# A fused attention and two feed-forward layers: another order of the first batch's ten attention groups

## Chip, cores and metric

One core of a Trainium2 chip runs the whole program. The metric is device time in microseconds (us), from the first to the last instruction of one execution. The engines are TensorE (PE; PEld is its weight load), VectorE (DVE), ScalarE (ACT), GpSimd (POOL), and SyncE (SP), which here only issues transfers.

## The reference

Attention with two kinds of heads (four look back 32 positions, four look at every 32nd position), then two gated feed-forward layers; only the first of them normalises its input.

```python
scores = q @ k^T / sqrt(64)                      # 4 batches, 8 heads, 576 positions, head width 64
mask_local   = (rel >= 0) & (rel < 32)           # heads 0..3
mask_strided = (rel >= 0) & (pos_k % 32 == pos_q % 32)   # heads 4..7
x = softmax(where(mask, scores, -1e9)) @ v       # as 2304 tokens of width 512
xn = x / sqrt(mean(x*x) + 1e-6) * rms_g
y = (silu(xn @ w_gate) * (xn @ w_val)) @ w_out   # 512 -> 1536 -> 512
out = (silu(y @ w_gate2) * (y @ w_val2)) @ w_out2
```

## The kernel before

**Attention.** A batch is worked in ten groups: five strided (numbers 0 to 4) and five local (5 to 9). Local groups 5 and 6 hold tokens 0 to 255 of the batch for the two pairs of heads, 7 and 8 hold tokens 256 to 511, 9 holds the last 64. Each group has three steps, in the diff called s, t and v. The step s (`local_s`, `strided_s`, `softmax_step`) makes the scores on PE, then the masked scores and row maxima on DVE (line 677), the exponentials on ACT (line 686), sums and reciprocals on DVE (lines 696 and 697) and the normalised tile `e` on POOL (line 703). The step t (`turn_step`) turns `e` on PE (line 80) and copies it to the tile `pT` on ACT (line 87). The step v (`local_v`, `strided_v`) multiplies by v on PE and copies the result to the token tile `x` on ACT (line 87).

**Normalisation.** `rms_step` makes the sums of squares over features of a piece of tokens on PE (`ones,ss`), the mean on DVE (868), the root on POOL (871), diagonal tiles `dg` on DVE (876), a broadcast on PE (`dg,ones`) and the scaled tokens on DVE (887). For batch 0 the first piece is its first 256 tokens (called r0 in the diff), the second the other 320 (r1). The first piece is then split into a high and a low part (`split`: `xh` on ACT at 998, `xl` on DVE at 999), and the feed-forward layer starts with segment 0, these 256 tokens.

**Order.** `batch` writes the steps as one list. Per place i of its loop it takes the scores of group i, the turn of group i-3 and the product of group i-4, so that three scores steps stand between the scores of a group and its turn. The loop `point` starts one step of the list at each of its calls, lets running steps advance by one phase, and between them starts phases of the weights' preparation. For a weight tile that is: load to `raw` (line 160), two ACT operations (288 and 280), two DVE operations (292 and 297), then a rounded half on ACT (305) and the rest on DVE (309). PE work is kept in the order written by hand (`traced`); ACT, DVE, POOL and SP are ordered by a scheduler from priorities.

**Fillers.** In the start phase `keep_busy` sets a given number of matmuls of a constant tile (`b_v<-warm`, line 72) ahead of some PE groups. Nothing uses their result. A table gives their number by the group's count.

**After the start.** Feed-forward chunks of segment 0 (gate `b_g<-xh,w`, value `b_v<-xh,w`, line 76) alternate on PE with the steps of batch 1, which came into the list behind batch 0. `silu` works on ACT at 975 and on DVE at 976; `hidden` is at 983 to 987.

Of the kernel before, what the change touches and what calls it, by code (L numbers as in the profile page):

```python
# [25 lines left out]
def attn_ffn_ffn(ctx: ExitStack, tc: tile.TileContext, q, k, v, w1g, w1v, w1o, rms_g, w2g, w2v, w2o, out):  # L26
# [7 lines left out]
    HC = FC // 3  # L34
# [32 lines left out]
    def keep_busy():  # L67
        if state["start"] and state["kind"] and state["group"] != state["filled"]:
            state["filled"] = state["group"]
            state["count"] += 1  # L70
            for _ in range({1: 26, 11: 34, 14: 16, 20: 6, 27: 8, 28: 5, 31: 7, 34: 9, 36: 22, 40: 2, 43: 5}.get(state["count"], 0)):
                traced(nc.tensor.matmul(att.fill, att.warm[:, :128], att.warm, start=True, stop=True))

    def product(out_, a, b_, start, stop, **how):
# [24 lines left out]
    state = {"rate": 640000.0, "slack": 0, "late": False, "xr": 0.6, "early": False, "start": True, "hold": False, "kind": "", "group": 0, "filled": 0, "count": 0, "lag": 3, "wait": 4}  # L99
# [211 lines left out]
    def weight_step(m, c, z, park=False):  # L311
        cell = {}
# [30 lines left out]
        def save():  # L343
# [5 lines left out]
            spent(cell["bk"], 6)  # L349
            parked[m, c, z] = d  # L350

        return Step([load] + [wait] * ((6, 6, 10, 6)[c] if (m, c) < (1, HC) else 0) + scale(cell, int(not park)) + ([high, low, save] if park else [first, second]),
                    lambda: (park or room[4]) and spaces() >= 1, PRIO_W)

    QUARTERS = ((1, 2), (5, 6), (7, 4), (3,))
# [139 lines left out]
    class Attention:  # L495
# [407 lines left out]
        def batch(self, b):  # L903
            groups = []
# [5 lines left out]
                               self.local_v(b, tiles, {3 if b else 1: 1, 4: 2}.get(i, 0))))  # L910
            res = []
            n = len(groups)
            for i in range(n + 4):
                if i == 0:
                    res += [self.strided_t(b, w, p, w and p == 2) for p in range(3) for w in range(2)]
                if i == 5:
                    res += [self.local_t(b, w, 0) for w in range(2)]
                if i == 5 + 0:
                    res += [self.local_t(b, w, 1) for w in range(2)] + [self.local_rest(b)]
                if i < n:  # L920
                    res.append(groups[i][0])
                if 0 <= i - 3 < n:
                    res.append(groups[i - 3][1])
                if 0 <= i - 4 < n:
                    res.append(groups[i - 4][2])
                    if i - 4 in (8 if b else 6, 9):
                        res.append(self.rms_step(b, int(i - 4 == 9)))
            return res

# [656 lines left out]
    for n, (m, cs, t0) in enumerate(work):  # L1586
# [54 lines left out]
        if n == 0:  # L1641
            cell = stage_x(nxt[0], nxt[2])
# [6 lines left out]
        for i, c in enumerate(chunks[:-1]):  # L1649
            c1 = chunks[i + 1]  # L1650
            step(c1, 1)
            if i == 0 and n and nxt:
                while due:
                    due.pop(0)[2]()
                cell = stage_x(nxt[0], nxt[2])
# [67 lines left out]
```

## Time and profile before

| | us |
|---|---|
| runs of before (three) | 999.80, 1001.33, 1003.00; median 1001.33 |
| profiled execution, its own time | 1004.73 |
| its span from first to last instruction | 1002.9 |
| PE busy in that span | 974.3 (97%) |
| ACT busy, DVE busy | 576.3, 580.5 |
| first feed-forward matmul on PE | 51.87 after the start |

The page of the profile divides the span into 40 slices of 25 us; the first two hold what the change touches. Within them the order of the single instructions on each engine counts, so the timelines of the engines are read, and a table of busy time by stretch.

### The profile page before, as it was taken

Reading aid. Unit: us, or ns where it says so; the run is one execution under the profiler, and the core shown is the slowest. Engines: PE = TensorE matmul, PEld = TensorE weight load, DVE = VectorE, ACT = ScalarE, POOL = GpSimd, SP = SyncE. Lnnn points to the kernel's source line nnn. Section 1 sums busy time; section 2 is a strip of 40 time slices with the busy share of each in tenths; the row PEclk is TensorE's granted clock in tenths of the full one; section 3 lists DMA queues with packets and bytes.
Section 4 is the critical chain, followed back from the end, with each engine's and each line's share of the span. In section 5 each row is a group of like instructions: output and inputs, shape, how many; then the busy total and the mean of one; then the engine's idle time right before and its main releaser. Section 6 shows DMA issues by size and latency. Waiting matters only on the chain.

```text
span 1002.9 us, 17802 instructions
## 1 busy us (share of the span) xinstructions
PE 974.3 (97%) x6054; PEld 897.0 (89%) x6054; DVE 580.5 (58%) x1319; ACT 576.3 (57%) x1465; POOL 387.4 (39%) x416
## 2 busy tenths in 40 slices
PE   9889998899999999899999999999999999999998
PEld 8778876678989999899999998999998999999997
DVE  5777768757335656356646657544556555663333
ACT  7988786755345645356555546555656645553431
POOL 3121254531221628161634565571516243441500
PEclk9989999999999999899999999999999999999999
DMA  7774669658684665887758685557887397955211
GB/s 199 225 214 141 165 188 265 207 190 286 225 290 153 208 201 190 309 269 240 247 178 280 232 253 219 186 188 274 288 281 260 110 327 242 324 179 168 88 60 63
DMA packets 168455, 215.89 MB, mean 215 GB/s; under 512 B 46860, under 2 KB 122028, under 8 KB 168364
## 3 DMA queue, kind: packets, MB, share of 16 engines
q1 hardware_dynamic: 158559, 199.48, 61.2%
q10 hardware_dynamic: 9805, 15.27, 4.2%
q8 instruction: 48, 0.79, 0.3%
q14 instruction: 43, 0.35, 0.1%
HBM read 142.87 MB, written 71.83 MB: 214 GB/s over the span
## 4 chain that ended last, share of the span: by engine, by line
PE 70%; DMA 4%; ACT 2%; DVE 1%; issue 0%; SPq 0%; DVEq 0%
PE b_y L76 32%; PE b_a L76 17%; PE b_g L76 12%; PE b_v L76 10%; DMA pk<-dh 1%; DMA w<-pk 1%; DMA raw<-in_moe_w_gate_dram 1%; DMA pk<-raw 0%; DMA xraw<-x_d 0%; SPq L160 0%; DMA part<-ob 0%; ACT xh L1395 0%; ACT dh L280 0%; DMA x_d<-x 0%; DVE dh L297 0%
## 5 line engine op out<-in xcount | busy, mean ns | idle before, releaser
L1396 POOL TENSOR_TENSOR xl<-xst,xh 128x384 fp32r<-128x384 f32 x196 | 211.3, 1099 | 178.8 <-PE b_y L76 77.7
L76 PE MATMUL b_y<-xh,w 128*128 128x384 f32 x784 | 211.6, 335 | 2.3 <-ACT t L1453 1.2
L76 PEld LDWEIGHTS b_y<-xh,w 128*128 128x128 f32 x784 | 142.9, 188 | 5.4 <-ACT t L1453 1.8
L76 PE MATMUL b_a<-xh,w 128*128 128x384 f32 (+2 forms) x512 | 141.1, 335 | 0.8 <-ACT t L1453 0.8
L76 PE MATMUL b_y<-xl,w 128*128 128x384 f32 x392 | 131.4, 335 | 0.0
L76 PE MATMUL b_g<-xh,w 128*128 128x384 f32 (+2 forms) x416 | 128.2, 350 | 1.2 <-DVE sg L976 1.2
L76 PE MATMUL b_v<-xh,w 128*128 128x384 f32 (+2 forms) x352 | 108.7, 352 | 3.6 <-ACT t L1467 3.6
L76 PEld LDWEIGHTS b_a<-xh,w 128*128 128x128 f32 x512 | 93.3, 188 | 4.1 <-ACT t L1453 1.8
L1395 ACT CAST xh<-xst 128x384 fp32r<-128x384 f32 x196 | 91.5, 520 | 0.0
L386 POOL TENSOR_TENSOR raw<-dh 128x256 f32<-128x256 f32 x40 | 29.4, 754 | 154.0 <-DVE dh L297 55.4
L76 PE MATMUL b_a<-xl,w 128*128 128x384 f32 (+2 forms) x256 | 85.9, 335 | 0.0
L76 PEld LDWEIGHTS b_g<-xh,w 128*128 128x128 f32 x416 | 77.8, 192 | 6.8 <-DVE sg L976 1.4
L76 PE MATMUL b_y<-hh,w 128*128 128x384 f32 (+2 forms) x304 | 81.4, 343 | 0.0
L76 PEld LDWEIGHTS b_y<-xl,w 128*128 128x128 f32 x392 | 73.6, 188 | 1.8
L76 PEld LDWEIGHTS b_v<-xh,w 128*128 128x128 f32 x352 | 65.5, 192 | 9.0 <-ACT t L1467 3.9
L76 PE MATMUL b_g<-xl,w 128*128 128x384 f32 (+2 forms) x208 | 70.8, 340 | 0.0
L703 POOL TENSOR_TENSOR e<-e,rc 128x384 f32<-128x384 f32 (+3 forms) x40 | 37.4, 940 | 84.3 <-DVE rc L697 15.9
L76 PE MATMUL b_y<-w,hh 128*128 128x512 f32 x216 | 67.1, 391 | 0.0
L686 ACT ACTIVATE e<-e,nb 128x96 f32<-128x96 f32 (+2 forms) x152 | 57.3, 386 | 8.0 <-DVE nb L677 8.0
L76 PE MATMUL b_v<-xl,w 128*128 128x384 f32 (+2 forms) x176 | 59.9, 340 | 0.0
L76 PEld LDWEIGHTS b_y<-hh,w 128*128 128x128 f32 x304 | 55.3, 190 | 2.8 <-ACT hh L986 0.2
L1473 DVE TENSOR_TENSOR b_y<-b_y,t 128x384 f32<-128x384 f32 x56 | 31.6, 565 | 43.1 <-ACT b_y L1467 42.1
(210 smaller groups left out, 2160.3 us busy)
## 6 DMA issues: line engine op xcount, KB each, us to landing
w<-pk SPq DMA_DIRECT2D x48, 512.0 KB
raw<-in_moe_w_gate_dram SPq DMA_DIRECT2D x24, 512.0 KB
raw<-in_moe_w_val_dram SPq DMA_DIRECT2D x24, 512.0 KB
raw<-in_moe_w_out_dram SPq DMA_DIRECT2D x24, 512.0 KB
pk<-raw ACTq DMA_DIRECT2D x48, 256.0 KB
part<-ob SPq DMA_DIRECT2D x48, 256.0 KB
xst<-y_d SPq DMA_DIRECT2D x30, 384.0 KB
xst<-xq SPq DMA_DIRECT2D x28, 384.0 KB
```

The costliest lines, as they stand in the source:

```text
L76: traced(nc.tensor.matmul(out_, a, b_, start=start, stop=stop, **how))
L386: paced(nc.gpsimd.tensor_tensor(out=t[:, z], in0=a, in1=b, op=ALU.subtract))
L686: r = nc.scalar.activation(out=e[:qn, i, :kn], in_=e[:qn, i, :kn], func=AF.Exp, bias=nb[:qn, i:i + 1], scale=-1.0, accum_out=sums[:qn, i:i ...
L703: eng.tensor_tensor(out=e[:qn, :nt, :kn], in0=e[:qn, :nt, :kn], in1=rc[:qn, :nt].unsqueeze(2).to_broadcast([qn, nt, kn]), op=ALU.mult)
L1395: nc.scalar.copy(out=xh[:, kk], in_=src[:, kk])
L1396: paced(nc.gpsimd.tensor_tensor(out=xl[:, kk], in0=src[:, kk], in1=xh[:, kk].bitcast(F32), op=ALU.subtract), ("pe", None))
L1473: nc.vector.tensor_tensor(out=s, in0=s, in1=v, op=ALU.mult)
```

## The change

The first batch gets an order of its own, written as a string. Places between scores and turns shrink: the turns and products of groups 0 to 6 follow each other closely, the scores of groups 8 and 9 stand behind the product of group 6 and the normalisation of the first piece (r0), and groups 7 to 9 end the list. The other three batches keep the loop. The fillers' table is changed from its sixth entry on (118 of them in all in place of 140), and a weight tile's number of waits for chunk 3 falls from 6 to 4.

```diff
-            for _ in range({1: 26, 11: 34, 14: 16, 20: 6, 27: 8, 28: 5, 31: 7, 34: 9, 36: 22, 40: 2, 43: 5}.get(state["count"], 0)):
+            for _ in range({1: 26, 11: 34, 14: 16, 20: 6, 27: 4, 28: 6, 30: 14, 33: 4, 37: 4, 39: 4}.get(state["count"], 0)):
...
-        return Step([load] + [wait] * ((6, 6, 10, 6)[c] if (m, c) < (1, HC) else 0) + scale(cell, int(not park)) + ([high, low, save] if park else [first, second]),
+        return Step([load] + [wait] * ((6, 6, 10, 4)[c] if (m, c) < (1, HC) else 0) + scale(cell, int(not park)) + ([high, low, save] if park else [first, second]),
...
             n = len(groups)
+            if b == 0:
+                res += [self.strided_t(b, w, p, w and p == 2) for p in range(3) for w in range(2)]
+                for word in "s0 s1 s2 s3 t0 s4 t1 v0 L s5 t2 v1 s6 t3 v2 t4 v3 t5 v4 t6 v5 s7 v6 r0 s8 s9 t7 v7 t8 v8 t9 v9 r1".split():
+                    if word == "L":
+                        res += [self.local_t(b, w, p) for p in range(2) for w in range(2)] + [self.local_rest(b)]
+                    elif word[0] == "r":
+                        res.append(self.rms_step(b, int(word[1])))
+                    else:
+                        res.append(groups[int(word[1])]["stv".index(word[0])])
+                return res
             for i in range(n + 4):
...
-                    if i - 4 in (8 if b else 6, 9):
+                    if i - 4 in (8, 9):
```

Three places show how the instructions move. In the names, `e` is a normalised tile, so a matmul `ident,e` is a turn; `pT,vs` and `pT,vl` are products of strided and local groups; `kT,qT` are scores.

On PE in the middle of the first batch, before (from the fillers ahead of the turn of group 4; repeated rows of scores left out):

```order
L72 MATMUL b_v<-warm 128x256 x8
L80 MATMUL b_y_633<-ident,e 108x108 x4
L72 MATMUL b_v<-warm 128x256 x5
L76 MATMUL b_y_658<-pT,vs_125 64x108 x4
L76 MATMUL b_a_678<-kT_479,qT_471 64x96
L80 MATMUL b_g<-ident,e 96x128 x4
L72 MATMUL b_v<-warm 128x256 x7
L76 MATMUL b_y_710<-pT,vs_125 64x108 x4
L76 MATMUL b_y_731<-kT_479,qT_471 64x96
L80 MATMUL b_y_759<-ident,e 96x128 x4
L72 MATMUL b_v<-warm 128x256 x9
L76 MATMUL b_a_769<-pT,vl_256 64x64 x8
```

On PE at the same place now, from the turn of group 4 to the scores of group 7:

```order
L80 MATMUL b_y_614<-ident,e 108x108 x4
L72 MATMUL b_v<-warm 128x256 x4
L76 MATMUL b_y_624<-pT,vs_125 64x108 x4
L72 MATMUL b_v<-warm 128x256 x6
L80 MATMUL b_y_640<-ident,e 96x128 x4
L76 MATMUL b_y_657<-pT,vs_125 64x108 x4
L72 MATMUL b_v<-warm 128x256 x14
L80 MATMUL b_a_666<-ident,e 96x128 x4
L76 MATMUL b_a_705<-pT,vl_256 64x64 x8
L76 MATMUL b_g<-kT_479,qT_471 64x96
```

The scores of groups 8 and 9 (`b_a_678`, `b_y_731`) are gone from between the turns, and those of group 7, ahead of the turn of group 4 before, now follow the product of group 5.

On ACT at the split of the first 256 tokens, before. The `qT` and `kT` rows copy what PE turned for batch 1; `raw` and `dh` belong to the weights of chunk 2:

```order
L998 CAST xh<-x_460 128x256
L87 COPY kT_954<-b_y_946 128x504
L998 CAST xh<-x_460 128x256
L288 ACTIVATE raw<-raw 128x512
L87 COPY qT_944<-b_y_956 128x432
L288 ACTIVATE raw<-raw 128x512 x2
L280 ACTIVATE dh<-raw 128x512 x2
L87 COPY kT_954<-b_a_969 128x432
```

On ACT at the same place now:

```order
L1008 CAST xh<-x_460 128x256
L87 COPY qT_921<-b_y_916 128x504
L1008 CAST xh<-x_460 128x256
L288 ACTIVATE raw<-raw 128x512 x2
L280 ACTIVATE dh<-raw 128x512 x2
L288 ACTIVATE raw<-raw 128x512
L87 COPY kT_928<-b_y_923 128x504
L87 COPY qT_921<-b_y_930 128x432
```

The first `kT` copy of batch 1 stood ahead of the last `xh` and of all five weight operations; now it stands behind them.

On DVE where the second strided group of batch 1 (126 rows) gets its reciprocal, before:

```order
L696 TENSOR_SCALAR sums<-sums 126x4
L983 SCALAR_TENSOR_TENSOR sg<-sg,b_v 128x256
L696 TENSOR_SCALAR sums<-sums 108x4
L297 SCALAR_TENSOR_TENSOR dh<-dh,raw 128x512
L697 RECIPROCAL rc<-sums 126x4
```

On DVE at the same place now (the scores' row stands four times, once shown):

```order
L993 SCALAR_TENSOR_TENSOR sg<-sg,b_v 128x256
L696 TENSOR_SCALAR sums<-sums 126x4
L677 ISA e,nb<-b_y_1160,ms 108x108
L696 TENSOR_SCALAR sums<-sums 108x4
L297 SCALAR_TENSOR_TENSOR dh<-dh,raw 128x512
L697 RECIPROCAL rc<-sums 126x4
```

The masked scores of the fifth strided group have come in ahead of this reciprocal, while the two reciprocal rows still stand behind the weights' row 297.

## Rows read from the trace of the kernel before

**Rows 1.** The page: busy us, share of the span and instructions of each engine.

```profile
PE 974.3 (97%) x6054; PEld 897.0 (89%) x6054; DVE 580.5 (58%) x1319; ACT 576.3 (57%) x1465; POOL 387.4 (39%) x416
```

**Rows 2.** Busy time by stretch: us, engines' busy us, then PEclk, DMA share, GB/s.

```profile
30.00:42.00 12.00, 10.14 (x118) 8.80 (x116) 8.54 (x34) 12.00 (x47) 3.81 (x5) 1.00 0.75 212
51.87:60.00 8.13, 6.65 (x58) 5.27 (x56) 7.98 (x35) 8.13 (x24) 1.15 (x2) 1.00 0.91 223
64.31:70.60 6.29, 6.29 (x28) 5.69 (x28) 3.99 (x21) 4.89 (x20) 4.33 (x4) 0.50 0.95 300
80.00:140.00 60.00, 59.43 (x618) 50.86 (x610) 43.12 (x189) 48.11 (x182) 19.71 (x23) 1.00 0.54 157
```

**Rows 3.** ACT timeline, 30 to 52: start, us, operation, idle before and its releaser.

```profile
31.55 0.39 ACT L686 ACTIVATE e<-e,nb 128x96 f32<-128x96 f32 x1
31.91 0.39 ACT L686 ACTIVATE e<-e,nb 128x96 f32<-128x96 f32 x1
...
34.42 0.70 ACT L280 ACTIVATE dh<-raw 128x512 f32<-128x512 f32 x1
34.98 0.69 ACT L288 ACTIVATE raw<-raw 128x512 uint32<-128x512 uint32 x1
35.53 0.55 ACT L87 COPY x<-b_y 128x108 f32<-128x108 f32 x2
35.85 0.66 ACT L305 CAST w<-dh 128x512 fp32r<-128x512 f32 x1
...
42.46 0.60 ACT L87 COPY pT<-b_y 96x512 f32<-96x512 f32 x1
42.92 0.65 ACT L305 CAST w<-dh 128x512 fp32r<-128x512 f32 x1
...
46.92 0.54 ACT L87 COPY x<-b_a 128x256 f32<-128x256 f32 x2 [0.83 <-PE b_a L76]
47.49 0.83 ACT L845 ACTIVATE sq<-x 128x320 f32<-128x320 f32 x2
49.51 0.41 ACT L998 CAST xh<-x 128x256 fp32r<-128x256 f32 x1 [1.19 <-DVE x L887]
...
50.90 0.58 ACT L87 COPY kT<-b_y 128x504 f32<-128x504 f32 x1
51.37 0.41 ACT L998 CAST xh<-x 128x256 fp32r<-128x256 f32 x1
```

**Rows 4.** PE timeline, 38 to 69, the same columns.

```profile
38.81 2.88 PE L72 MATMUL b_v<-warm 128*128 128x256 f32 x22
43.11 0.77 PE L76 MATMUL b_g<-pT,vl 96*64 96x64 f32 x16 [1.42 <-ACT pT L87]
...
51.53 0.56 PE L80 MATMUL b_y<-ident,kn 108*64 108x108 f32 x4 [0.45 <-ACT kT L87]
51.87 0.36 PE L76 MATMUL b_g<-xh,w 128*128 128x256 f32 x1
...
62.30 0.39 PE L76 MATMUL b_g<-xh,w 128*128 128x256 f32 x1 [1.22 <-DVE sg L976]
...
64.31 1.10 PE L80 MATMUL b_y<-ident,e 126*126 126x126 f32 x4 [1.38 <-POOL e L703]
...
68.49 1.04 PE L80 MATMUL b_a<-ident,e 126*126 126x126 f32 x4
```

**Rows 5.** DVE timeline, 49 to 66.

```profile
49.00 1.65 DVE L887 SCALAR_TENSOR_TENSOR x<-x,gcol,b_g 128x256 f32<-128x256 f32 x4
...
54.16 0.27 DVE L677 CUSTOM_DVE_ANT_0 e<-b_y,ms 126x126 f32<-126x126 f32 x1
...
56.80 1.91 DVE L887 SCALAR_TENSOR_TENSOR x<-x,gcol,b_a 128x320 f32<-128x320 f32 x4
...
65.53 0.23 DVE L697 RECIPROCAL rc<-sums 126x4 f32<-126x4 f32 x2
```

**Rows 6.** POOL timeline, 65 to 70.

```profile
65.86 3.54 POOL L703 TENSOR_TENSOR e<-e,rc 126x504 f32<-126x504 f32 x3 [1.61 <-DVE sums L696]
```

## Prediction

> **What bounds the kernel now.** I read the page first: PE is busy 97% of the span, ACT and DVE 57 and 58% [rows 1]. That says that an end saved or lost at the start reaches the result only if it moves the PE work behind it. So next the table by stretch [rows 2]. From 80 to 140 us PE is busy 59.43 of 60.00, at its full clock of 2.4 GHz: from there on PE is the bound. In the first batch it is not. From 30 to 42 ACT is busy 12.00 of 12.00 and a good part of PE's time is fillers. From 51.87 to 60.00 ACT (8.13 of 8.13) and DVE (7.98) bound, and PE has only 6.65. From 64.31 to 70.60 PE is busy throughout, but at a granted clock of 0.50, which is 1.2 GHz, so it does 3.1 us of full-clock work in 6.29. The question is then when PE reaches its dense stretch, around 68 to 70 us, and at which clock.
>
> Third, the timelines of the single engines. On ACT [rows 3] instructions follow each other without a gap until 46; the copy of a turned tile at 42.46 is what PE waits for until 43.11 [rows 4], after 2.88 us of fillers and 1.42 idle. After that ACT has two gaps, 0.83 and 1.19, in which the normalisation of the first piece runs alone [rows 3]. The scaled tokens start on DVE at 49.00 [rows 5], the first feed-forward matmul at 51.87, held until then by a turn of batch 1 that waited for a `kT` copy on ACT [rows 4].
>
> **The change, part by part.** Prices are distances from one start to the next, since an ACT row is longer than what it keeps the engine for: an exponential 0.36, a weight operation 0.56, a pair of x copies 0.32, a pT copy 0.46 (0.60 until its reader may start), a kT copy 0.47, all from [rows 3]; a cast of 0.66 by the same overlap 0.53; two 256-column x copies 0.54.
>
> *Products of groups 3 to 6 come earlier, scores of 7 to 9 later.* Until 32.59 ACT's order is the old one (the exponential at 31.91, one more distance of 0.36, one pair of copies). From there to the end of group 9's exponentials it now has: 10 exponentials 3.60, 3 pT copies 1.38, 2 pairs of x copies 0.64, 2 x copies 0.54, 4 weight operations 2.24, 3 casts 1.59, and the squares of 576, twice 288 and twice 256 columns, by the 0.83 for twice 320 some 2.16. Sum 12.15, so 44.7 us, if nothing waits. What was to become shorter, the way from the product of group 6 to the tokens' norm, thus still stands behind the same ACT work. All of this is order, not work; nothing is removed but fillers.
>
> *The tail.* Behind the exponentials the last three groups run as a chain between ACT and PE: pT of group 7 (0.60, to 45.3), its product (0.77 by the row at 43.11, to 46.1), four fillers (2.88 / 22 = 0.13 each, to 46.6), turn of group 8 (0.56, as the turn at 51.53, to 47.2), pT (0.60, to 47.8), product (0.77, to 48.6), half a turn for group 9 (0.3) and the broadcast, bounded by a turn's half, 0.3. On PE the broadcast stands behind the product of group 8 and the turn of group 9, so the scaled tokens start at 49.1 to 49.2. Before: 49.00. The mean, the root and the diagonal tiles are hidden under that chain. The shorter places win nothing here: the gain of 2.0 (the two ACT gaps) is given back as gaps of the ping-pong.
>
> *The first feed-forward matmul.* The first `xh` comes 0.51 behind the scaling [rows 3, 5], at 49.7. Before, 2.17 us lay from there to the first weight operation (49.51 to 51.37 and 0.31 of cast); now one kT copy less (0.47) and two squares more (0.75): to 52.1. Then five weight operations, 2.8, to 54.9, and only then the kT copy, 0.58, to 55.5. The last turn of batch 1 writes the bank that this copy empties, and in PE's order it stands ahead of the first feed-forward matmul by 0.34 [rows 4]. So that matmul starts at about 55.8, against 51.87: 3.9 later. Most of this is covered: ACT and DVE have no gap there [rows 2], and the weight operations had to be done anyway. If that cover is gone, it costs its 3.9.
>
> The Trainium skill, "PSUM — Partial Sum Buffer", section "Engine vs sequencer instructions", says that the queues of VectorE, ScalarE and GpSimdE are strictly first in, first out. By that rule the kT copy cannot pass the weight operations, and the matmul starts at 55.8; without it the copy could go at once and the matmul would start at about 52.5. The trace agrees: the pT copy at 42.46 of [rows 3] kept PE idle 1.42.
>
> *Batch 1's groups.* Their scores follow three feed-forward matmuls (0.4): 56.2. The scores themselves I bound by 0.4 and by four times 0.36, and take 0.6, since pairs run on both halves of the array: 56.8. The first maximum on DVE takes 0.2 [rows 5], four exponentials 1.44, sums and reciprocal 0.3: 58.8. DVE now does this before it scales the second piece (1.91 from 56.80 before [rows 5]), so that starts at 58.8 and ends at 60.7. From there DVE came to the reciprocals of group 1 of batch 1 in 6.82 (58.71 to 65.53), without a gap. Now the fifth group's four maxima stand ahead of them (4 x 0.21 = 0.84) and a sum and a reciprocal (0.3) have gone ahead: 7.3. The reciprocal comes at 68.0, 2.5 later. POOL takes 0.33 to start and 3.54 / 3 = 1.18 for the tile [rows 5, 6]: 69.5. The turn of group 1 of batch 1 then starts on PE at 69.6, against 68.49 [rows 4]: **1.1 later**.
>
> *Clock.* Before, PE idled 1.22 and 1.38 within 61 to 64.31, and the clock stood at 0.50 from 64.31 to 70.60 [rows 2, 4], of which 2.1 us lie behind the turn at 68.49 and cost 1.05. Now the turn of group 0 comes at about 63.4 (DVE is 2.3 behind the end of the scaling with `sg`, then three matmuls); the work to the next turn was 4.18 at half clock, 2.1 at full, so PE idles some 4 us ahead of 69.6. If the clock stays up, 1.05 is won; if it falls in that gap and stays down 6.29 as before, up to 2 us more lie behind the turn, 1.0 lost. I take zero, the clock being as much down there as before.
>
> *Fillers and waits.* 22 fillers less are 2.9 us of PE time, all beside ACT work: nothing. The two waits fewer make up for fewer calls of `point` in the shorter list; no more is moved by them than two weight operations of chunk 3: nothing to 0.6.
>
> **Sum.** +1.1 + 0 + 0 against the profiled execution's own 1004.73 gives 1005.8; the three runs' median lies 3.4 below that execution, so 1002.4. Bounds of the sum are 0 and +2.7: 1001.3 to 1004.0.
>
> **Rivals.** *Slower: a second stretch at half clock.* At about 50 to 55.5 PE has only transposes and then waits for the kT copy; if the clock falls there, the first chunk's gate and value and batch 1's scores run at 1.2 GHz, and the later gap makes it fall again. Price: 3.1 for a stretch such as that of 64.31 to 70.60, and 1.0 for the longer second one, on top of 1.1: +5.2, 1006.5. It decides from the point where the granted clock between 50 and 58 reads 0.50. For it: before, the clock fell after gaps of 1.22 and 1.38, and those that I find here are longer; against it, ACT and DVE bound there, and would hide part of it. The Trainium skill, "TensorE: Matmul & The Clock Gate", section "HAM oscillation — how this bites in real kernels", tells of kernels whose waits between bursts bring the throttle back each time. By that rule this rival holds.
>
> *Faster.* The tail could come out shorter than I add it up: if DVE has `dg` early and the broadcast is not held by group 8, the scaling starts 1.3 earlier (the product and the fillers gone from the chain), and if PE, starting later but denser, avoids the half clock at 64.31, that gives 3.1: -4.4, 996.9. For it: before, nothing ran beside the norm for 2.0. Against it: the DVE order above.
>
> *Nothing arrives.* The transfers and the other batches' chains behind 140 us may take up a shift of 1 us: 1001.3.
>
> **How the numbers follow.** The forecast, 1002.4, has 0.45; nothing arrives 0.12; the second half clock 0.23; faster 0.20. The forecast's own range is 1001.3 to 1004.0. About 0.3% (3 us) is what a measurement can tell from no change. So faster by more 0.20, within it 0.57, slower by more 0.23. The range from 997.2 to 1006.2 leaves out the outer halves of the two rivals.
>
> **What would show it.** Right: exponentials of group 9 end near 44.7, scaled tokens near 49.1, first feed-forward matmul near 55.8 behind a kT copy that follows five weight operations, the turn of group 1 of batch 1 near 69.6. Wrong: a first feed-forward matmul before 53; that turn before 68; a clock of 1.00 all through 60 to 72 (faster) or of 0.50 already at 52 to 58 (slower).

## The result and the profile of the changed kernel

The changed kernel takes 1007.54 us, the median of 6 runs; the kernel before takes 1000.57 on the same chip. The ratio is 1.0072 with a 95% interval of 1.0049 to 1.0094. It is slower by 7.0 us, where I forecast 1002.4 with a range up to 1006.2. Its profiled execution took 1008.8 us, with a span of 1007.0.

The first view is busy time by stretch, in the columns of [rows 2]:

```profile
30.00:42.00 12.00, 8.24 (x120) 6.82 (x120) 8.04 (x26) 12.00 (x40) 1.64 (x3) 0.96 0.79 226
42.00:52.00 10.00, 8.46 (x58) 7.26 (x58) 3.84 (x20) 5.03 (x20) 2.82 (x5) 0.50 0.45 137
52.00:60.00 8.00, 5.95 (x42) 5.36 (x41) 7.00 (x20) 7.23 (x18) 2.50 (x2) 0.71 0.56 147
60.00:70.00 10.00, 10.00 (x70) 8.45 (x70) 7.30 (x37) 6.76 (x27) 1.03 (x1) 0.75 0.84 202
70.00:80.00 10.00, 6.43 (x44) 5.58 (x44) 7.46 (x34) 7.34 (x30) 4.40 (x4) 0.83 0.79 238
80.00:140.00 60.00, 58.97 (x594) 50.72 (x595) 44.17 (x180) 47.73 (x167) 13.35 (x16) 1.00 0.49 136
```

In 30 to 42 ACT is busy throughout, as before [rows 2], but PE only 8.24 us where it was 10.14. Then comes what the forecast did not have: the granted clock is 0.50, 1.2 GHz, all through 42 to 52, and stays low for most of the time up to 80. From 80 on PE is dense at full clock, as before. So the loss was made ahead of 80 us. On PE's timeline (start, us, operation, idle before and its releaser) one sees where:

```profile
31.57 0.59 PE L76 MATMUL b_y<-pT,vs 108*64 108x108 f32 x8 [1.67 <-ACT pT L87]
...
39.93 0.80 PE L76 MATMUL b_y<-pT,vl 96*64 96x64 f32 x16 [1.80 <-ACT pT L87]
...
42.79 1.09 PE L80 MATMUL b_g<-ident,e 128*96 128x128 f32 x4 [1.18 <-POOL e L703]
...
47.80 1.06 PE L80 MATMUL b_y<-ident,e 128*96 128x128 f32 x4
49.52 1.12 PE L76 MATMUL b_y<-pT,vl 96*64 96x64 f32 x16 [0.67 <-ACT pT L87]
...
58.79 0.93 PE L80 MATMUL b_y<-ident,kn 108*64 108x108 f32 x4 [1.71 <-ACT kT L87]
59.41 0.56 PE L76 MATMUL b_g<-xh,w 128*128 128x256 f32 x1
...
75.29 1.10 PE L80 MATMUL b_a<-ident,e 126*126 126x126 f32 x4 [3.57 <-POOL e L703]
```

Ahead of 43 us PE idles 1.67, 1.80 and 1.18 us, for the weighted values of groups 3 and 6 and the turn of group 7. The stretches of half a microsecond around 41 (columns of [rows 2]) tell where the clock falls, and so does the window from the first of these waits on:

```profile
31.57:41.00 9.43, 7.63 (x112) 6.50 (x116) 6.20 (x19) 9.43 (x32) 0.83 (x1) 1.00 0.79 234
40.50:41.00 0.50, 0.50 (x23) 0.43 (x23) 0.00 (x0) 0.50 (x5) 0.00 (x0) 1.00 0.65 165
41.00:41.50 0.50, 0.50 (x20) 0.32 (x12) 0.14 (x1) 0.50 (x3) 0.00 (x0) 0.52 0.56 169
```

It falls at 41, behind the first two waits; the third, 1.18 us up to 42.79, begins after the fall. The wait of 1.80 stands ahead of the product of group 6. That is the place where the kernel before has its 22 fillers [rows 4]; the change leaves 4 there. The turn at 42.79 takes 1.09 us; in x_hole, below, the same turn takes 0.64 at full clock. The tail behind it, a chain between ACT and PE, runs at half clock. The first feed-forward matmul starts at 59.41 instead of 51.87 [rows 4], and the turn of group 1 of batch 1 at 75.29 instead of 68.49.

ACT in the same execution, and in the second fence DVE:

```profile
44.42 0.36 ACT L686 ACTIVATE e<-e,nb 128x96 f32<-128x96 f32 x1
44.78 0.56 ACT L87 COPY pT<-b_g 96x512 f32<-96x512 f32 x1
...
55.35 1.26 ACT L288 ACTIVATE raw<-raw 128x512 uint32<-128x512 uint32 x2
56.50 1.22 ACT L280 ACTIVATE dh<-raw 128x512 f32<-128x512 f32 x2
57.61 0.68 ACT L288 ACTIVATE raw<-raw 128x512 uint32<-128x512 uint32 x1
58.16 0.58 ACT L87 COPY kT<-b_y 128x504 f32<-128x504 f32 x1
```

```profile
52.13 1.65 DVE L887 SCALAR_TENSOR_TENSOR x<-x,gcol,b_a 128x256 f32<-128x256 f32 x4 [4.53 <-PE b_a L76]
...
73.53 0.24 DVE L697 RECIPROCAL rc<-sums 126x4 f32<-126x4 f32 x2
```

The exponentials of group 9 end at 44.78, where I had 44.7, and the kT copy does stand behind five weight operations. But the scaled tokens start at 52.13, not at 49.1: DVE idled 4.53 us, waiting for PE's broadcast. The reciprocals of group 1 of batch 1 come at 73.53, where I had 68.0.

That the delay stays is seen at the first scaled tokens of batch 1 on DVE, in the kernel before, in the changed kernel, and in z_all, the changed kernel with its idle stretches filled (third series):

```profile
106.36 2.45 DVE L887 SCALAR_TENSOR_TENSOR x<-x,gcol,b_a 128x448 f32<-128x448 f32 x4 [0.58 <-PE b_a L76]
114.22 2.45 DVE L887 SCALAR_TENSOR_TENSOR x<-x,gcol,b_a 128x448 f32<-128x448 f32 x4 [0.58 <-PE b_a L76]
108.08 2.46 DVE L887 SCALAR_TENSOR_TENSOR x<-x,gcol,b_a 128x448 f32<-128x448 f32 x4 [0.58 <-PE b_a L76]
```

The changed kernel is 7.9 us behind the kernel before there, about the whole loss; z_all is 1.7 behind.

### The profile page after: what moved, and what is told of

Same layout as the page of the kernel before. It is cut to its first block, busy times and chain, and to the rows that moved or that the text cites. A ratio compares the mean times of both kernels' runs of the same rounds, so it can differ in the third digit from the quotient of the medians.

```text
span 1007.0 us, 17754 instructions
## 1 busy us (share of the span) xinstructions
PE 977.0 (97%) x6032; PEld 899.0 (89%) x6032; DVE 581.0 (58%) x1319; ACT 577.1 (57%) x1465; POOL 387.7 (38%) x416
## 4 chain that ended last, share of the span: by engine, by line
PE 71%; ACT 2%; DMA 2%; DVE 1%; issue 0%; SPq 0%; DVEq 0%
PE b_y L76 33%; PE b_a L76 17%; PE b_g L76 12%; PE b_v L76 10%; DMA pk<-dh 1%; DMA raw<-in_moe_w_gate_dram 1%; DMA xraw<-x_d 0%; ACT xh L1405 0%; ACT dh L280 0%; DVE dh L297 0%; ACT hh L1487 0%; ACT raw L288 0%; ACT t L1463 0%; ACT t L1477 0%; DVE hl L997 0%
```

## Experiments

**How they are read.** Two theories. *Clock*: the loss comes from the half clock, which begins because PE has longer idle stretches in the new order with fewer fillers. *Order*: it comes from where instructions now stand on ACT and DVE. The table gives for each kernel the mean granted clock of 40 to 75 us, the start of the scaled tokens, of the first feed-forward matmul and of the turn of group 1 of batch 1 (each from its one profiled execution, us), and the ratio to the kernel before, timed on the same chip. A single execution stands for its kernel only in part: the mean granted clock over a whole execution, on record for every run (a fall anywhere in the 1000 us counts in it), differs between executions of one kernel (0.984 to 0.993 in the ten of y_thin). An execution as a whole can also be shifted: in the old order the last exponential of the first batch ended at 39.3 in one and at 41.1 in another, in the new order between 44.7 and 46.4.

| kernel | clock 40 to 75 | scaled | first matmul | turn | ratio, 95% |
|---|---|---|---|---|---|
| before | 0.90 | 49.00 | 51.87 | 68.49 | 1 |
| changed | 0.71 | 52.13 | 59.41 | 75.29 | 1.0072 (1.0049 to 1.0094) |
| a_filled | 0.90 | 49.80 | 55.90 | 70.75 | 1.0042 (1.0025 to 1.0060) |
| a_late_w | 0.72 | 53.63 | 58.72 | 72.40 | 1.0134 (1.0101 to 1.0166) |
| a_filled_late_w | 0.90 | 49.84 | 55.58 | 70.16 | 1.0113 (1.0087 to 1.0139) |
| b_thin | 0.71 | 51.81 | 55.05 | 71.30 | 1.0041 (1.0023 to 1.0060) |
| x_hole | 0.76 | 50.73 | 58.00 | 73.16 | 1.0052 (1.0031 to 1.0073) |
| x_order | 0.71 | 52.36 | 58.96 | 73.76 | 1.0074 (1.0048 to 1.0099) |
| x_all | 0.97 | 49.92 | 57.67 | 71.93 | 1.0087 (1.0059 to 1.0115) |
| y_thin | 0.90 | 51.98 | 54.85 | 70.26 | 1.0028 (1.0013 to 1.0043) |
| z_all | 1.00 | 49.28 | 56.16 | 70.57 | 1.0001 (0.9985 to 1.0016) |
| z_filled_all | 1.00 | 49.34 | 54.44 | 68.37 | 1.0012 (0.9990 to 1.0035) |
| z_late | 1.00 | 50.60 | 53.47 | 68.89 | 1.0022 (1.0002 to 1.0042) |
| waits6 | 0.71 | 52.63 | 59.91 | 75.64 | 1.0132 (1.0102 to 1.0161) |
| only_last | 0.71 | 53.73 | 61.02 | 76.41 | 1.0043 (1.0025 to 1.0061) |
| all_but_last | 0.92 | 50.24 | 57.11 | 71.55 | 1.0040 (1.0019 to 1.0060) |
| z_all_w6 | 1.00 | 49.56 | 56.43 | 70.88 | 1.0053 (1.0035 to 1.0072) |
| b_waits4 | 0.90 | 50.60 | 53.48 | 70.09 | 0.9990 (0.9972 to 1.0008) |
| kT_22 | 0.93 | 49.55 | 57.30 | 71.56 | 1.0050 (1.0028 to 1.0071) |
| open_329 | 0.90 | 50.25 | 58.47 | 72.73 | 1.0058 (1.0039 to 1.0077) |

### First series: the table of fillers and the weights

**a_filled**, the changed kernel with more fillers in its table:

```diff
-            for _ in range({1: 26, 11: 34, 14: 16, 20: 6, 27: 4, 28: 6, 30: 14, 33: 4, 37: 4, 39: 4}.get(state["count"], 0)):
+            for _ in range({1: 26, 11: 34, 14: 16, 20: 6, 27: 16, 28: 6, 30: 14, 33: 17, 36: 9, 37: 4, 39: 4}.get(state["count"], 0)):
```

> The changed kernel with three of its table's entries raised: 16 instead of 4 fillers ahead of the weighted values of group 3, 17 instead of 4 ahead of those of group 6, 9 instead of none ahead of the turn of group 7, so that the idle stretches of 1.67, 1.80 and 1.18 us on TensorE ahead of 42.8 us are closed. Theory 'clock' (the lost microseconds come from the half clock that begins at 41 to 42 us): granted clock 1.00 in 40 to 50, scaled tokens (DVE, L887) at 49.1 to 49.6 instead of 52.13, first feed-forward matmul at 55.6 to 56.2 instead of 59.41, the turn of group 1 of batch 1 at 71 to 72.5 instead of 75.29, time 3 to 4 us under the changed kernel, ratio to the kernel before 1.002 to 1.005. Rival 'order' (the loss comes from where instructions stand on ScalarE, and the clock is only a sign of it): the clock is 1.00 but the first feed-forward matmul stays at 58 or later, and the ratio stays at 1.006 to 1.008.

The first matmul came at 55.90 and the ratio at 1.0042, as the clock theory had it, with a clock of 1.00 in 40 to 50. But the edit was not clean: the planner counts fillers as time and had answered by moving rows on ACT and DVE. The kT copy now stood at 52.54, ahead of the weight operations. The test was made again without that, below.

**a_late_w** moves the weight steps of chunk 2 instead, and **a_filled_late_w** does both:

```diff
-        return Step([load] + [wait] * ((6, 6, 10, 4)[c] if (m, c) < (1, HC) else 0) + scale(cell, int(not park)) + ([high, low, save] if park else [first, second]),
+        return Step([load] + [wait] * ((6, 6, 13, 4)[c] if (m, c) < (1, HC) else 0) + scale(cell, int(not park)) + ([high, low, save] if park else [first, second]),
```

> The changed kernel with 13 waits instead of 10 ahead of the weight steps of chunk 2, so that one instead of five weight operations stands ahead of the copy of the first kT of batch 1 on ScalarE; fillers as in the changed kernel. Theory 'clock': the clock falls at 41 to 42 us as before, scaled tokens at 52.1 as in the changed kernel; of the 6.5 us from the first split copy (52.93) to the first feed-forward matmul (59.41) some 2.7 go, so that it stands at 56.5 to 57; time 2 to 3 us under the changed kernel, ratio 1.004 to 1.006. Rival 'order': nearly all goes, ratio 1.000 to 1.002. Third possibility: the weights of chunk 2 come too late for their own matmuls, and nothing is won, ratio 1.007 or more.

> Both edits: the closed idle stretches and the 13 waits. If the two causes are separate and add, scaled tokens at 49.1 to 49.6, the first feed-forward matmul at 52.3 to 53.3 (the kernel before: 51.87), ratio 0.999 to 1.002. If the clock is the only cause, as the kernel with the closed stretches alone; if the order is the only one, as the kernel with the 13 waits alone.

Both were much slower, 1.0134 and 1.0113: the third possibility. On PE's timeline of a_late_w the feed-forward matmul of that chunk waits for its own weights:

```profile
88.55 0.58 PE L76 MATMUL b_g<-xh,w 128*128 128x256 f32 x1 [3.93 <-ACT w L305]
```

In a_filled_late_w the same wait is 3.96 us. So the five weight operations ahead of the kT copy are not there for nothing: they can't be put off without being missed at 85 us.

**b_thin**, the kernel before with one hole in its fillers, 4 in place of 22 ahead of the product of group 6, the number that the changed kernel has there:

```diff
-            for _ in range({1: 26, 11: 34, 14: 16, 20: 6, 27: 8, 28: 5, 31: 7, 34: 9, 36: 22, 40: 2, 43: 5}.get(state["count"], 0)):
+            for _ in range({1: 26, 11: 34, 14: 16, 20: 6, 27: 8, 28: 5, 31: 7, 34: 9, 36: 4, 40: 2, 43: 5}.get(state["count"], 0)):
```

> The kernel before with 4 instead of 22 fillers at the one place where its TensorE waits longest (ahead of the weighted values of group 7, 38.81 to 43.11 us), so that the idle stretch there grows from 1.42 to some 3.6 us. Theory 'clock': the clock falls to 0.50 from about 43 us in the old order too, scaled tokens 1.5 to 3 us later than 49.00, ratio 1.002 to 1.005. Rival 'order' (the old order does not mind a half clock at this place): ratio 0.999 to 1.001 though the clock falls. If the clock stays at 1.00, this one stretch does not decide it and nothing moves.

1.0041, with the clock at 0.62 in 40 to 50. The old order minds a half clock at this place as well. Here too the planner had moved rows, so it was repeated as y_thin.

### Second series: fillers put into the finished program

From here on fillers were added to, or taken from, the program after the planner had ordered it: `change` says how many stand ahead of the n-th matrix instruction. Every other instruction keeps its place on every engine.

```diff
+def refill(nc, change):
+    block = [b for b in nc.m.functions[0].blocks if b.name.endswith("_kernel")][0]
...
+            for i in range(max(k, 0)):
...
+                out.append(type(ins)(start_tensor_calc=True, stop_tensor_calc=True, tile_size=spare.tile_size, tile_position=spare.tile_position,
+                                     name=f"I-{900000 + 100 * n + i}", engine=spare.engine, ins=spare.ins, outs=outs, debug=spare.debug, sync_info=info))
```

In the changed kernel, 199 is the product of group 3 with its values, 255 that of group 6, 275 the turn of group 7, 283 the sums of the mean, 301 the product of group 8, 329 the sums of the second mean, 340 the turn that waits for the kT copy, 404 the turn of group 1 of batch 1.

**x_hole** and **x_order**. The first is the changed kernel with a_filled's fillers, the second a_filled with them taken out at the same three places:

```diff
+    refill(nc, {199: 12, 255: 13, 275: 9})
```

```diff
+    refill(nc, {211: -12, 280: -13, 309: -9})
```

> The changed kernel with 34 fillers put into its finished program (12 ahead of the weighted values of group 3, 13 ahead of those of group 6, 9 ahead of the turn of group 7), so that every other instruction keeps its place on every engine; in the kernel a_filled the planner had answered the same fillers with 28 moved rows on ScalarE and 42 on VectorE. Theory 'clock': granted clock 1.00 in 40 to 50, scaled tokens at 49.1 to 49.8, the first kT copy of batch 1 still behind five weight operations, first feed-forward matmul at 55.6 to 56.3 as forecast; the time falls by 3 to 4 us, ratio 1.002 to 1.005. Rival 'order': a_filled gained by its moved rows and not by its clock; then the ratio stays at 1.006 to 1.008 here.

> The other half: the finished program of a_filled (its order on ScalarE and VectorE, with the kT copy ahead of the weight operations) with the 34 fillers taken out again, so that the idle stretches are those of the changed kernel. Theory 'clock': the clock falls at 41 to 42 us, scaled tokens at 52 to 52.6, first feed-forward matmul at 57.5 to 58.5, ratio 1.006 to 1.009. Rival 'order': ratio 1.003 to 1.005 as in a_filled.

x_order came out at 1.0074, so a_filled's moved rows alone bring nothing, and the 34 fillers are worth 0.3% in that order (1.0074 against 1.0042). x_hole came out at 1.0052, 0.2% under the changed kernel and 0.1% over a_filled, within the intervals of both, and its first matmul stood at 58.00, not at 56. The stretches by 10 us and the product of group 8 show what its profiled execution did; the last line is the same product in a_filled:

```profile
40.00:50.00 10.00, 8.06 (x105) 6.96 (x106) 4.94 (x25) 7.06 (x30) 2.91 (x5) 0.88 0.73 208
50.00:60.00 10.00, 9.44 (x53) 7.97 (x51) 7.68 (x20) 7.85 (x19) 1.31 (x2) 0.50 0.60 152
```

```profile
48.12 1.12 PE L76 MATMUL b_y<-pT,vl 96*64 96x64 f32 x16 [0.67 <-ACT pT L87]
```

```profile
48.27 0.69 PE L76 MATMUL b_y<-pT,vl 96*64 96x64 f32 x16 [0.67 <-ACT pT L87]
```

With the first three stretches closed the clock fell some 7 us later, at 48, behind idle stretches of 0.90 and 0.67. a_filled has stretches of 0.91 and 0.67 at the same places, and there it held (0.69 us for the same product). In x_hole half clock then covers 50 to 60. But this is one execution of each. Over whole executions x_hole's five read 0.984 to 0.990, the profiled one the lowest, and a_filled's ten 0.985 to 0.991; so it is not shown that the two programs differ at this place, nor that this fall is what kept x_hole from winning more.

**x_all** closes the following stretches as well:

```diff
+    refill(nc, {199: 12, 255: 13, 275: 9, 283: 6, 301: 5, 340: 22})
```

> As x_hole, with the stretches behind it closed too: 6 fillers ahead of the sums of the mean, 5 ahead of the weighted values of group 8, 22 ahead of the last turn of kn of batch 1 (the wait on the kT copy). Theory 'clock': granted clock 1.00 up to 60; the first feed-forward matmul still at 55.5 to 56.2, since it waits for the copies and not for TensorE, but the stretch behind it runs at full clock and the turn of group 1 of batch 1 stands at 69.5 to 71 (forecast 69.6); ratio 1.000 to 1.003. If the fillers ahead of the kT copy stand in the way of what waits behind them, 1.004 or more.

A miss: the clock was 1.00 up to 70, but 4 runs gave 1.0087. Its profiled execution was the fastest of the four, 1007.2 us. It left two stretches open, 1.47 us at 53.2 and 3.57 ahead of the turn of group 1, and its 22 fillers ended 0.9 us behind the kT copy. Over the whole execution its clock reads 0.991, that of the other three 0.986 to 0.989. The fourth and fifth series return to it.

**y_thin** is b_thin without moved rows; in the kernel before, 294 is the product of group 6, by the order of the products on PE (the expectations call it group 7's):

```diff
+    refill(nc, {294: -18})
```

> The kernel before with 18 of the 22 fillers ahead of the weighted values of group 7 taken out of its finished program, all else in its place (in b_thin the planner moved 17 rows on ScalarE and 37 on VectorE as well). Theory 'clock': half clock from 43 us, scaled tokens at 51 to 52, ratio 1.002 to 1.005. Rival 'order': the loss of b_thin came from its moved rows, ratio 0.999 to 1.001.

```profile
44.89 0.92 PE L76 MATMUL b_g<-pT,vl 96*64 96x64 f32 x16 [3.55 <-ACT pT L87]
```

```profile
40.00:50.00 10.00, 6.45 (x86) 5.49 (x82) 5.60 (x13) 8.25 (x25) 2.15 (x3) 0.83 0.63 192
```

One idle stretch of 3.55 us instead of 1.42 [rows 4], nothing else moved, and the ratio is 1.0028 (1.0013 to 1.0043). So 18 fillers at this place, 2.2 us of work that computes nothing, are worth 2.8 us (1.3 to 4.3) to the kernel before. The time shows this, the trace does not show the path: measured from the last exponential of the first batch, the scaled tokens come 1.2 us later than in the kernel before, the turn of group 1 no later (29.12 against 29.15). The profiled execution, with a mean granted clock of 0.991 over its whole length, is one of three at 0.991 to 0.993; the other seven read 0.984 to 0.986.

### Third series: everything closed

**z_all** closes every stretch of the changed kernel up to 75 us; 404 writes the bank that the turn behind it overwrites, and waits for its last reader:

```diff
+    refill(nc, {199: 12, 255: 13, 275: 9, 283: 6, 301: 5, 329: 10, 340: 13, 404: (24, True, 130)})
```

> The changed kernel's finished program with every idle stretch of TensorE up to 75 us closed by fillers, nothing else moved: the six of x_all (13 instead of 22 ahead of the wait on the kT copy, which had run 0.9 us too long), 10 ahead of the sums of the second mean, and 24 ahead of the turn of group 1 of batch 1, where the changed kernel idles 3.57 us. Theory 'clock alone': granted clock 1.00 from 30 to 80 and a ratio of 0.999 to 1.002. Theory 'clock and order' (x_hole and x_all suggest it): clock 1.00, scaled tokens at 49.9, first feed-forward matmul at 56.7 to 57.3, the turn of group 1 at 71 to 71.6, some 3 us behind the kernel before, ratio 1.003 to 1.005.

The ratio is 1.0001 (0.9985 to 1.0016): with no instruction moved but fillers added, the 7 us are gone. Stretches and PE's timeline:

```profile
42.00:52.00 10.00, 9.53 (x103) 8.47 (x102) 6.47 (x28) 7.16 (x27) 2.71 (x5) 1.00 0.64 184
52.00:60.00 8.00, 7.71 (x68) 6.75 (x66) 6.07 (x25) 7.07 (x20) 2.50 (x2) 1.00 0.80 199
60.00:70.00 10.00, 9.16 (x75) 8.01 (x73) 9.60 (x53) 9.46 (x39) 1.87 (x2) 1.00 0.85 217
70.00:80.00 10.00, 9.43 (x96) 8.51 (x96) 7.53 (x22) 8.05 (x21) 3.56 (x4) 1.00 0.58 187
```

```profile
56.16 0.36 PE L76 MATMUL b_g<-xh,w 128*128 128x256 f32 x1
...
66.84 3.03 PE L72 MATMUL b_a<-warm 128*128 128x256 f32 x24
70.57 0.65 PE L80 MATMUL b_a<-ident,e 126*126 126x126 f32 x4 [0.70 <-POOL e L703]
```

and DVE and ACT:

```profile
49.28 1.66 DVE L887 SCALAR_TENSOR_TENSOR x<-x,gcol,b_a 128x256 f32<-128x256 f32 x4 [1.78 <-PE b_a L76]
```

```profile
54.61 0.69 ACT L288 ACTIVATE raw<-raw 128x512 uint32<-128x512 uint32 x1
55.18 0.59 ACT L87 COPY kT<-b_y 128x504 f32<-128x504 f32 x1
```

The clock reads 1.00 in every stretch. Over whole executions it is 0.982 to 0.984 in all six of the changed kernel, 0.993 to 0.997 in all twelve of z_all, and 0.988 to 0.995 in the 29 of the kernel before that were timed with z_all. DVE's wait for the broadcast is 1.78 us instead of 4.53, and the kT copy still stands behind its five weight operations. The order theory falls as an explanation of the 7 us. It does not follow that the order is free: the kernel before, against which z_all is even, has a half-clocked stretch of its own, which z_late takes up.

**z_filled_all** does the same in a_filled's order, ahead of the sums of the mean, the product of group 8, the sums of the second mean and the turn of group 0 of batch 1:

```diff
+    refill(nc, {317: 6, 335: 5, 363: 10, 424: (20, True, 0)})
```

> The order of a_filled (kT copy ahead of the weight operations; the reciprocal of group 0 behind the split operations) with its remaining idle stretches closed as well: 6 fillers ahead of the sums of the mean, 5 ahead of the weighted values of group 8, 10 ahead of the sums of the second mean, 20 ahead of the turn of group 0 of batch 1 (idle 2.84 us there). Theory 'clock and order': clock 1.00 from 30 to 80, first feed-forward matmul at 54.3 to 54.9 instead of 55.90, the turn of group 0 at 66.5 to 67.5 instead of 68.41, ratio 1.001 to 1.004 (a_filled: 1.0042). Theory 'clock alone': ratio 0.999 to 1.001.

1.0012 (0.9990 to 1.0035), no difference that these runs can tell from z_all, though its first matmul comes 1.7 us earlier. Its 0.3% against a_filled are the fillers' alone, with a clock of 0.90 there and 1.00 here.

**z_late** asks whether the kernel before loses by its own half clock of 64.31 to 70.60 [rows 2]; 412 is the turn of group 0 of batch 1 there:

```diff
+    refill(nc, {412: (10, True, 0)})
```

> The kernel before, its finished program, with 10 fillers ahead of the turn of group 0 of batch 1 (idle 1.38 us there, and the half clock of 64.31 to 70.60 begins there). If a half clock costs wherever it stands: clock 1.00 in 60 to 70, the turn of group 1 at 66.5 to 67.5 instead of 68.49, 1 to 3 us won, ratio 0.997 to 0.999. If the half clock there is covered by the waits on GpSimd's normalization: clock 1.00, turn of group 1 at 68, ratio 0.999 to 1.001. If the clock falls all the same: nothing, ratio 1.000.

```profile
60.00:70.00 10.00, 7.95 (x61) 6.71 (x59) 9.54 (x53) 10.00 (x43) 3.94 (x3) 1.00 0.86 234
140.00:180.00 40.00, 34.88 (x258) 27.29 (x257) 31.07 (x102) 28.08 (x89) 15.12 (x18) 0.91 0.89 259
```

The clock is 1.00 there, and by the times nothing is won: 1.0022 (1.0002 to 1.0042). In the profiled execution, measured from the last exponential of the first batch, the turn of group 1 came 1.2 us earlier (27.95 against 29.15 us) and the first scaled tokens of batch 1 2.2 us earlier (64.85 against 67.02). Where this gain goes is open. The clock of 140 to 180 reads 0.91, in the kernel before 0.96, but over 140 to 200 it reads 0.94 in both.

By the times z_all (1.0001) is no slower than z_late (1.0022), so the new order at full clock costs nothing that they can tell against the old one; in the traces z_late's first scaled tokens of batch 1 start 2.3 us ahead of z_all's (105.79 against 108.08). So a price of the order of some 2 us is not ruled out.

**waits6** undoes the second part of the change:

```diff
-        return Step([load] + [wait] * ((6, 6, 10, 4)[c] if (m, c) < (1, HC) else 0) + scale(cell, int(not park)) + ([high, low, save] if park else [first, second]),
+        return Step([load] + [wait] * ((6, 6, 10, 6)[c] if (m, c) < (1, HC) else 0) + scale(cell, int(not park)) + ([high, low, save] if park else [first, second]),
```

> The changed kernel with the second part of the change undone: 6 waits instead of 4 ahead of the weight steps of chunk 3. The forecast gave it nothing to 0.6 us. Up to 75 us the rows stand as in the changed kernel, and the half clock from 41 us with them; ratio 1.005 to 1.008, as the changed kernel. If the 4 waits carry a part of the loss, 1.003 or less; if they carry a gain, 1.009 or more.

1.0132: the 4 waits are worth 6 us in the new order, where I had priced them at nothing to 0.6.

### Fourth series: which stretch, and the waits

**only_last** and **all_but_last** split z_all's fillers in two:

```diff
+    refill(nc, {404: (24, True, 130)})
```

```diff
+    refill(nc, {199: 12, 255: 13, 275: 9, 283: 6, 301: 5, 329: 10, 340: 13})
```

> The changed kernel's finished program with the 24 fillers ahead of the turn of group 1 of batch 1 and no others, so that only its last idle stretch (3.57 us) is closed and the half clock from 41 to 65 us stands. Theory 'the whole clock': the rows up to 71 us as in the changed kernel, the clock 1.00 in 70 to 80, and the 1 to 2 us that the half clock of 75.3 to 78.6 costs are won: ratio 1.004 to 1.007. Theory 'the last stretch decides' (x_all, without these fillers, 1.0087; z_all, with them, 1.0001): ratio 0.999 to 1.002.

> z_all without the 24 fillers ahead of the turn of group 1 of batch 1: full clock up to 73 us, then the idle 3.57 us and half clock behind it. Theory 'the whole clock': 1 to 2 us over z_all, ratio 1.001 to 1.003, and x_all's 1.0087 came from its 22 fillers ahead of the kT copy, which stood in the way. Theory 'the last stretch decides': ratio 1.006 to 1.009, as x_all.

1.0043 and 1.0040. Against the changed kernel the last stretch alone brings 0.29%, all the others 0.32%, and together 0.71%: they add within their intervals, which are wide (0.2% to either side). So the last stretch does not decide alone. Nor does the start of the turn of group 1 tell the end: from the end of the first batch's exponentials to it, it is 30.0 us in only_last against 30.5 in the changed kernel, and 25.9 in all_but_last as in z_all; what differs within each pair is the clock behind the turn. The clock of 40 to 50 and of 70 to 80, first in only_last, then the latter in all_but_last:

```profile
40.00:50.00 10.00, 7.76 (x75) 6.90 (x76) 6.02 (x33) 7.33 (x30) 2.91 (x5) 0.59 0.79 239
...
70.00:80.00 10.00, 9.63 (x81) 8.74 (x81) 9.60 (x40) 8.62 (x38) 4.26 (x4) 1.00 0.84 258
```

```profile
70.00:80.00 10.00, 8.45 (x57) 7.70 (x57) 5.18 (x13) 6.04 (x19) 4.41 (x4) 0.69 0.57 178
```

**z_all_w6** is waits6 with z_all's fillers, and **b_waits4** the kernel before with 4 waits:

```diff
-        return Step([load] + [wait] * ((6, 6, 10, 6)[c] if (m, c) < (1, HC) else 0) + scale(cell, int(not park)) + ([high, low, save] if park else [first, second]),
+        return Step([load] + [wait] * ((6, 6, 10, 4)[c] if (m, c) < (1, HC) else 0) + scale(cell, int(not park)) + ([high, low, save] if park else [first, second]),
```

> z_all's fillers in the program with 6 waits instead of 4 ahead of the weight steps of chunk 3 (waits6: 1.0132 against 1.0072 of the changed kernel). If the 4 waits only mend what the half clock breaks, nothing moves at full clock: ratio 0.999 to 1.002. If they carry a gain of their own in the new order, 1.004 to 1.008, and in 90 to 100 us the granted clock falls as in waits6 (0.66).

> The kernel before with the second part of the change alone: 4 waits instead of 6 ahead of the weight steps of chunk 3. By the forecast nothing (0 to 0.6 us): ratio 0.999 to 1.001. If the earlier weight operations win in the old order what they win in the new one (6 us), 0.994 to 0.996; if they take ScalarE's time from the exponentials of batch 1, 1.002 to 1.005.

With full clock up to 80 us the two waits still make 0.5% in the new order (1.0053 against 1.0001), and in the old order no difference that can be told (0.9990, 0.9972 to 1.0008). PE in z_all_w6 shows what they are for:

```profile
83.11 0.39 PE L76 MATMUL b_g<-xh,w 128*128 128x256 f32 x1 [1.56 <-ACT w L305]
...
85.14 0.40 PE L76 MATMUL b_g<-xh,w 128*128 128x256 f32 x1 [1.53 <-DVE w L309]
```

With 6 waits the feed-forward matmuls wait twice for weights that are made too late; z_all has no such wait. Behind the waits the clock falls too: 0.83 in 80 to 90, against 1.00 in z_all.

### Fifth series: x_all's odd result

```diff
+    refill(nc, {199: 12, 255: 13, 275: 9, 283: 6, 301: 5, 329: 10, 340: 22})
```

```diff
+    refill(nc, {199: 12, 255: 13, 275: 9, 283: 6, 301: 5, 340: 13})
```

> all_but_last with 22 instead of 13 fillers ahead of the wait on the kT copy, as x_all had them. If fillers that run past the copy's end delay the path one for one (9 x 0.12 = 1.1 us, less what the wait still held): 0.5 to 1.1 us over all_but_last, ratio 1.0045 to 1.0055. If they are what lies between all_but_last (1.0040) and x_all (1.0087): 1.007 to 1.010. If nothing: 1.003 to 1.005.

> all_but_last without the 10 fillers ahead of the sums of the second mean, so that the idle 1.47 us of x_all stands there. If the clock falls behind it (53 us), the copies and scores of batch 1 run at half clock: first feed-forward matmul 0.5 to 1.5 us later than 57.11 and ratio 1.005 to 1.008. If one such stretch among dense work does not bring the clock down: 1.003 to 1.005.

The first, **kT_22**, gave 1.0050, the second, **open_329**, 1.0058, both a little above all_but_last's 1.0040 and within its interval. From the end of the first batch's exponentials to the first feed-forward matmul it is 11.5 us in all_but_last, 12.3 in kT_22 and 12.8 in open_329. In open_329 the clock fell behind the open stretch:

```profile
53.53 0.78 PE L76 MATMUL b_a<-ones,ss 128*128 128x1 f32 x6 [1.47 <-DVE ss L846]
```

```profile
50.00:60.00 10.00, 8.52 (x67) 7.78 (x67) 7.89 (x23) 7.89 (x19) 2.50 (x2) 0.83 0.67 168
```

x_all has both faults. Their sum, 0.10% and 0.18% on top of 0.40%, makes 1.007, inside x_all's interval (1.0059 to 1.0115). That each of them costs is not settled by these times, and x_all's own trace is against the second: its stretch of 1.47 us left the clock at 1.00 up to 70. Its odd result stays open.

## Why the prediction was wrong

**The step that failed is the clock's.** I wrote "I take zero, the clock being as much down there as before", and of the fillers "all beside ACT work: nothing". The runs put 7 us there: 1.0072 with the idle stretches, 1.0001 without them, in the same order. The part behind the gap ahead of the last turn, for which I allowed at most 1.0, is 2.9 us of it (only_last, give or take as much); the stretches ahead of it, which have no term in my sum, are 3.2 (all_but_last).

I had looked for half clock only from 50 us on, where my rival stood, and priced every PE instruction of the tail at its full-clock duration. The fall came at 41, ahead of that tail. The signs were in the rows: 22 fillers stood ahead of the product of group 6 and a wait of 1.42 [rows 4], with the clock at 1.00 in that stretch [rows 2], and I read them as PE time that costs nothing instead of asking what the clock does without them. The change took 18 of them away at that product, and the clock fell just behind it; y_thin answers for the old order: the same 18 are worth 2.8 us. (The table changes from its fifth entry on, not from its sixth.)

The Trainium skill, "TensorE: Matmul & The Clock Gate", section "HAM oscillation — how this bites in real kernels", describes bursts of matmuls divided by waits, each of which brings the throttle back. I cited it for the rival at 50 us; the trace agrees with it 9 us earlier, with a granted clock of 0.50 in 42 to 52, in so far as the clock fell between waits. It does not agree on each: the wait of 1.67 us ahead of 31.57 left the clock at 1.00, and it fell behind that of 1.80.

**Step by step.** The column of z_all is the changed order at full clock, which is what my sum assumed up to the last turn:

| step | forecast | z_all | changed |
|---|---|---|---|
| end of group 9's exponentials | 44.7 | 44.68 | 44.78 |
| scaled tokens | 49.1 | 49.28 | 52.13 |
| first feed-forward matmul | 55.8 | 56.16 | 59.41 |
| turn of group 1 of batch 1 | 69.6 | 70.57 | 75.29 |
| time against before | +1.1 us | +0.1 (-1.5 to +1.6) | +7.2 (+4.9 to +9.4) |

- *ACT without a gap to 44.7*: right, in both.
- *The tail*: right at full clock, within 0.2 us. At half clock it costs 2.85 more, and this goes on to the first matmul (3.25).
- *The kT copy behind five weight operations*: right. It has its price, 4.3 us between the first matmuls of z_all and of the kernel before. z_all is no slower than that kernel, so most of it is covered there, as I had it; against the old order at full clock this is open (z_late).
- *The turn at 69.6*: 1.0 too early at full clock. At half clock it came 4.7 later still. That its 1.1 us reach the end one for one is not borne out: z_all's turn comes 2.1 us later than before and its time is +0.1.
- *22 fillers less cost nothing*: wrong, as above.
- *Two waits less, nothing to 0.6*: by themselves they are worth 5 to 6 us in the new order and nothing that can be told in the old one. I had looked at which rows they move and not at when the feed-forward matmuls ask for those weights. That they make up for the shorter list, as I wrote, is what z_all_w6 shows, and so the sum, which has the 4 waits in it, was not spoiled.

**The rivals.** The one on the slower side, a second stretch at half clock, named the mechanism and came near in time (1006.5, measured 1007.54). Its place and deciding point were wrong: in 52 to 60 the clock reads 0.71; the fall had come at 41, and a part of that stretch was at full clock again. That it came near in time is in part luck: it priced a stretch that begins 9 us later. I gave it 0.23, weighing against it that ACT and DVE bound there and would hide part. In the tail they hide nothing: DVE waits 4.53 us for PE there. The rival on the faster side counted on 3.1 us from avoiding the half clock at 64.31; the times of z_late show nothing of them, though its trace keeps 2.2 us up to 106 us.

## What to carry to other kernels

Fillers that hold TensorE's clock belong to an order: whoever moves the order must look for the idle stretches anew, from the first instruction that moves, and give the old fillers' work a price. A half clock costs where a chain goes through TensorE and back (the tail here); one further on won nothing in the times when it was closed (z_late), and why is not shown. So each is to be tested by closing the stretch with nothing else moved, over many executions, since one profiled execution need not be like the others. And an edit that a planner sees is not one edit: the same 34 fillers moved some 70 rows of ACT and DVE when the planner knew of them, and none when they were put in behind it.

## What the runs showed of the hardware that I had not expected

- No idle stretch shortly ahead of the fall is longer than 1.80 us. Behind one of 1.47 among dense work the clock fell in open_329 (mean 0.83 in 50 to 60) and did not fall in x_all (1.00 up to 70). z_all held 1.00 with stretches of 0.7.
- Nearly equal programs can fall on different sides in single executions: with stretches of 0.90 and 0.67 x_hole fell to half clock at 48, with 0.91 and 0.67 at the same places a_filled did not. Executions of one kernel differ as well (0.984 to 0.990 over x_hole's five), so the stretches alone do not tell the outcome.
- The changed kernel was half-clocked all through 42 to 52, and its scaled tokens came 2.85 us later for it than z_all's; the kernel before is half-clocked in 64.31 to 70.60 and pays nothing that the times of z_late could show.
